# Storing the second feed-forward layer's weights unsplit, splitting left-over probabilities in two steps, and pooling one batch's values on TensorE

## The chip, the cores and the metric

The kernel runs on one core of a Trainium2 chip. The metric is the device time of one execution in microseconds (us); lower is better. TensorE (PE) multiplies matrices into PSUM, VectorE (DVE), ScalarE (ACT) and GpSimd (POOL) work on elements, and SyncE (SP) issues most DMAs from one queue, in order.

## The reference

Eight batches of 8 heads, 576 tokens and 64 dimensions each; keys and values are averaged over groups of 8 tokens before the attention. Then two feed-forward layers over all 4608 tokens.

```python
k_p = k.reshape(B, H, Sp, pool, D).mean(axis=3)
v_p = v.reshape(B, H, Sp, pool, D).mean(axis=3)
attn = softmax(scale * q @ k_p.T)
x = (attn @ v_p) reshaped to 4608 x 512
h = x @ w_in                       # 512 -> 2048
x = (s * relu(h)**2 + b) @ w_out   # 2048 -> 512
gate = sigmoid(x @ w_gate)         # 512 -> 1536
val = x @ w_val
out = (gate * val) @ w_out2        # 1536 -> 512
```

The weights arrive as 64-bit floats.

## The kernel before

Matrix products in 32-bit precision are made of three products of a rounded part and a remainder: `split(hi, lo, src, eng)` writes `hi` with an ACT copy (L55) and `lo = src - hi` with a subtraction (L56) on DVE or POOL. A product then takes three matmuls for each 128 rows (hi by lo, hi by hi, lo by hi).

**Start and attention.** Tokens go in units of 256. `scores` multiplies queries by pooled keys and leaves the difference from the maximum (L385, L386, both read PSUM on DVE); `norm` divides by the sum on POOL (L405); `left` splits the 8 left-over probabilities of each head into four slices, by two ACT copies (L412) and two DVE subtractions (L414); `turn` transposes on PE (L430, L436); `values` multiplies by the values (L448 to L451). Pooling of keys and values is a tree of POOL additions (`add`, L284; the last step of keys is L298), for batch 0 alone a sum of identity matmuls on PE (`pool_v_pe`, L326). Attention steps are spread over the first layer by a table `events`.

**First layer.** A loop over 144 steps: 9 blocks of 512 tokens by 16 slices of the hidden dimension. A step multiplies into `hps` (`emit_h`, L211 to L213) and accumulates a step two back into `acc` (`emit_x`, L242 to L244): 24 matmuls of 512 columns. In the first block the step also turns the 64-bit words of `w_in` and `w_out` into 32-bit floats: `convert` is one ACT row (L80) and three DVE rows (L81, L82, L83) for a slice, and a split on POOL follows.

**Preparation of the second layer.** From step 18 on, `prep_w2` does the same for the gate, value and output weights, one of nine parts per step, 12 slices in all. A load (`load64`, L67) takes one of three `raw` buffers; a store (L142) of a finished piece waits at the head of the SP queue until POOL has written it, and a `raw` buffer that a store reads is free for the next load only after it. Seven operand matrices (gate and value halves and four sums and differences, L187) leave for DRAM already split, as hi and lo.

**Second layer.** Two token blocks at a time, four pairs, then one block left over. `fetch_w7` loads the seven operands of a slice (L652) into one of two buffers, as soon as the matmuls on that buffer two slices back are done. `first_half` and `second_half` make seven products, 42 matmuls, with additions on DVE out of PSUM (L667), a sigmoid on ACT (L678), a multiplication (L679) and a split; `emit_o` multiplies by the output weights, 12 matmuls. PE's order is the program's order from step 16 on; the other engines' orders come from a scheduler.

Of the kernel before, what the change touches and what calls it, by code (L numbers as in the profile page):

```python
# [19 lines left out]
def pooled_attention_two_ffn(ctx, tc, q, k, v, v_left, w_in, w_out, s_in, b_in, w_gate, w_val, w_out2, out):  # L20
# [40 lines left out]
    w7d = [dram.tile([128, 2, 8 * 256], F32, name=f"w7d{m}") for m in range(M2)]  # L61
# [77 lines left out]
    def store_later():  # L139
        while later:  # L140
            dst, t = later.pop(0)
            nc.sync.dma_start(out=dst, in_=t.bitcast(F32))  # L142
# [18 lines left out]
    def store_split(dst, raw, src):  # L161
        n = src.shape[1]
        t = raw.rearrange("p (two f) -> p two f", two=2)[:, :, :n]
        split(t[:, 0].bitcast(F32R), t[:, 1].bitcast(F32R), src, nc.gpsimd)
        later.append((dst, t))

    def raw_tile():
        return rawp.tile([128, 1024], I32, tag="raw", name="raw")

    def prep_w2(m, part):  # L170
        h0, h1 = slice(0, 256), slice(256, 512)
        if part == 0:
            prep["g"] = load64(w_gate[m])
        elif part == 1:
            prep["v"] = load64(w_val[m])
        elif part == 2:
            raw = prep["g"]
            prep["gt"] = convert(raw, cv_tile())
            store_split(w7d[m][:, :, 256:768], raw, prep["gt"])
        elif part == 3:  # L180
            prep["vt"] = convert(prep["v"], cv_tile())
            store_split(w7d[m][:, :, 0:256], raw_tile(), prep["vt"][:, h0])
        elif part == 4:
            gt, vt, c = prep["gt"], prep["vt"], cv_tile().bitcast(F32)
            for o, a, b_, op in ((c[:, h1], gt[:, h0], vt[:, h0], ALU.subtract), (vt[:, h0], vt[:, h0], vt[:, h1], ALU.add),
                                 (c[:, h0], vt[:, h0], gt[:, h0], ALU.subtract), (gt[:, h1], gt[:, h1], c[:, h0], ALU.subtract)):
                nc.gpsimd.tensor_tensor(out=o, in0=a, in1=b_, op=op)  # L187
            prep["c"] = c
        elif part == 5:
            store_split(w7d[m][:, :, 768:1280], prep["v"], prep["vt"])  # L190
        elif part == 6:
            store_split(w7d[m][:, :, 1280:1792], raw_tile(), prep["c"])
        elif part == 7:
            store_split(w7d[m][:, :, 1792:2048], raw_tile(), prep["gt"][:, h1])
            prep["o"] = load64(w_out2[m])
        else:
            store_split(wo2d[m], prep["o"], convert(prep["o"], cv_tile()))
# [617 lines left out]
```

## Time and profile before

| | |
|---|---|
| median of 3 runs | 1815.9 us (1811.99 to 1817.01) |
| profiled execution, its own time | 1814.27 us |
| its span | 1812.5 us |
| mean granted TensorE clock | 0.985 |
| busy: PE, DVE, ACT, POOL | 96%, 53%, 38%, 20% |

The span runs from the first to the last instruction. A busy share is an average over stages that differ: the start and the conversion of the first layer's weights (to about 165 us), the rest of the first layer (to about 990 us), and the second layer.

### The profile page before, as it was taken

The page shows a single profiled execution, that of the slowest core. Times are in us where ns is not written, and L with a number is a line of the kernel's source. Part 1 is how long each engine was busy: PE and PEld are TensorE (multiplying, and loading weights), DVE is VectorE, ACT ScalarE, POOL GpSimd, SP SyncE. Part 2 cuts the span into 40 slices and gives each one's busy share as a digit, 9 for nine tenths or more (in the row PEclk, how much of TensorE's full clock was granted, in tenths as well). Part 3 has the DMA queues.
Part 4 walks back from the last instruction along what each step waited for, and adds up shares of the span by engine and source line. Part 5 has one row for each costly group of instructions (what it writes and reads, how often), then busy time and mean ns, then how long its engine had stood idle before and what let it go on. Part 6 is the DMA issues. An engine that isn't in the chain of part 4 may idle for free.

```text
span 1812.5 us, 21425 instructions
## 1 busy us (share of the span) xinstructions
PE 1741.0 (96%) x8032; PEld 1445.5 (80%) x8032; DVE 965.1 (53%) x1527; ACT 693.9 (38%) x1222; POOL 367.1 (20%) x395
## 2 busy tenths in 40 slices
PE   5788999999998989999999999999999999999999
PEld 4576877788887878888888888888888888888887
DVE  7997756656456665545352544455445544554111
ACT  2566544454454545445453222222222222222111
POOL 5754624406053241403000000000000000000000
PEclk7899999999999999999999999999999999999999
DMA  6676745747275553725345555855585558555764
GB/s 239 237 240 209 259 166 184 261 134 252 95 256 186 197 201 132 271 94 175 105 151 197 192 178 204 284 197 185 192 284 199 201 178 289 202 197 173 262 227 150
DMA packets 103095, 364.21 MB, mean 201 GB/s; under 512 B 10192, under 2 KB 17360, under 8 KB 102992
## 3 DMA queue, kind: packets, MB, share of 16 engines
q1 hardware_dynamic: 99792, 352.36, 56.7%
q0 software_dynamic: 3200, 10.49, 1.8%
q8 instruction: 63, 1.03, 0.2%
q14 instruction: 40, 0.33, 0.1%
HBM read 304.09 MB, written 58.72 MB: 200 GB/s over the span
## 4 chain that ended last, share of the span: by engine, by line
PE 73%; DVE 9%; DMA 8%; POOL 5%; issue 3%; ACT 2%; SPq 0%; POOLq 0%; DVEq 0%; ACTq 0%
PE acc L719 5%; PE pc L663 5%; PE pc L661 5%; PE acc L717 5%; PE pc L662 5%; PE acc L718 5%; PE hps L211 4%; PE hps L213 4%; PE hps L212 4%; PE acc L242 4%; PE pb L661 4%; PE pb L663 4%; PE pb L662 4%; PE acc L243 4%; PE acc L244 4%; DMA raw<-in 4%
## 5 line engine op out<-in xcount | busy, mean ns | idle before, releaser
L667 DVE TENSOR_TENSOR wk<-pc,wk 128x512 f32<-128x512 f32 x192 | 132.4, 690 | 240.7 <-PE pc L663 240.6
L211 PE MATMUL hps<-xl,wi 128*128 128x512 f32 (+1 forms) x584 | 236.8, 406 | 7.2 <-ACT wi L55 4.4
L242 PE MATMUL acc<-gl,woh 128*128 128x512 f32 x576 | 227.0, 394 | 11.0 <-DVE gl L56 11.0
L213 PE MATMUL hps<-xh,wi 128*128 128x512 f32 (+1 forms) x584 | 229.9, 394 | 0.0
L56 DVE TENSOR_TENSOR gl<-g,gh 128x512 fp32r<-128x512 f32 x204 | 160.2, 785 | 130.7 <-ACT gh L55 124.3
L212 PE MATMUL hps<-xh,wi 128*128 128x512 f32 (+1 forms) x584 | 229.3, 393 | 0.0
L244 PE MATMUL acc<-gh,wol 128*128 128x512 f32 x576 | 225.6, 392 | 0.0
L243 PE MATMUL acc<-gh,woh 128*128 128x512 f32 x576 | 225.5, 392 | 0.0
L55 ACT ACTIVATE gh<-g 128x512 fp32r<-128x512 f32 x204 | 128.2, 628 | 144.9 <-DVE g L679 142.1
L219 DVE TENSOR_TENSOR g<-g 128x512 f32<-128x512 f32 x128 | 101.7, 795 | 142.1 <-ACT g L215 142.0
L678 ACT ACTIVATE g<-pb 128x512 f32<-128x512 f32 x60 | 35.8, 597 | 347.7 <-PE pb L663 347.7
L661 PE MATMUL pc<-xo,w 128*128 128x512 f32 x432 | 168.0, 389 | 0.0
L662 PE MATMUL pc<-xo,w 128*128 128x512 f32 x432 | 168.0, 389 | 0.0
L663 PE MATMUL pc<-xo,w 128*128 128x512 f32 x432 | 168.0, 389 | 0.0
L568 POOL DMA_DIRECT2D cv<-x2d x36 | 19.5, 542 | 724.5 <-DMA out<-eo 338.3
L220 ACT ACTIVATE g<-g,b_sb,s_sb 128x512 f32<-128x512 f32 x144 | 117.1, 814 | 99.6 <-DVE g L219 98.4
L215 ACT ACTIVATE g<-hps 128x512 f32<-128x512 f32 x144 | 85.1, 591 | 154.5 <-PE hps L213 153.4
L242 PEld LDWEIGHTS acc<-gl,woh 128*128 128x128 f32 x576 | 108.8, 189 | 35.9 <-DVE gl L56 13.9
L211 PEld LDWEIGHTS hps<-xl,wi 128*128 128x128 f32 x584 | 112.5, 193 | 28.8 <-ACT wi L55 4.6
L213 PEld LDWEIGHTS hps<-xh,wi 128*128 128x128 f32 x584 | 111.8, 191 | 23.9
L661 PE MATMUL pb<-xo,w 128*128 128x512 f32 x336 | 130.7, 389 | 0.0
L662 PE MATMUL pb<-xo,w 128*128 128x512 f32 x336 | 130.7, 389 | 0.0
(109 smaller groups left out, 3331.0 us busy)
## 6 DMA issues: line engine op xcount, KB each, us to landing
w<-w7d SPq DMA_DIRECT2D x48, 1792.0 KB, 7.7
wi<-w1d SPq DMA_DIRECT2D x128, 512.0 KB, 3.7
wo<-wo2d SPq DMA_DIRECT2D x108, 512.0 KB, 4.4
raw<-in SPq DMA_DIRECT2D x68, 512.0 KB, 4.8
w7d<-raw SPq DMA_DIRECT2D x36, 512.0 KB, 3.6
w<-w7d SPq DMA_DIRECT2D x12, 1280.0 KB, 6.6
kv<-in SPq DMA_DIRECT2D x24, 512.0 KB, 6.0
kv<-in SPq DMA_DIRECT2D x16, 576.0 KB, 4.3
```

The costliest lines, as they stand in the source:

```text
L55: nc.scalar.activation(out=hi, in_=src, func=ACTF.Copy)
L56: eng.tensor_tensor(out=lo, in0=src, in1=hi.bitcast(F32), op=ALU.subtract)
L211: nc.tensor.matmul(out=ps[:, f], lhsT=hi[:, kk], rhs=c[:, kk, f], start=kk == 0, stop=False)
L212: nc.tensor.matmul(out=ps[:, f], lhsT=hi[:, kk], rhs=a[:, kk, f], start=False, stop=False)
L213: nc.tensor.matmul(out=ps[:, f], lhsT=lo[:, kk], rhs=a[:, kk, f], start=False, stop=kk == KD - 1)
L242: nc.tensor.matmul(out=acc[j][d], lhsT=hi[:, f], rhs=gl, start=m == 0, stop=False)
L243: nc.tensor.matmul(out=acc[j][d], lhsT=hi[:, f], rhs=gh, start=False, stop=False)
L244: nc.tensor.matmul(out=acc[j][d], lhsT=lo[:, f], rhs=gh, start=False, stop=m == M1 - 1)
L661: nc.tensor.matmul(out=ps, lhsT=w[:, 0, x, kk], rhs=r[:, 1, kk, :n], start=first and kk == 0, stop=False, skip_group_check=True)
L662: nc.tensor.matmul(out=ps, lhsT=w[:, 0, x, kk], rhs=r[:, 0, kk, :n], start=False, stop=False, skip_group_check=True)
L663: nc.tensor.matmul(out=ps, lhsT=w[:, 1, x, kk], rhs=r[:, 0, kk, :n], start=False, stop=kk == 1, skip_group_check=True)
L667: nc.vector.tensor_tensor(out=o, in0=ps, in1=b_, op=ALU.add)
```

## The change

It has three parts. The seven operands of the second layer are kept in DRAM as plain 32-bit floats: `gt` and `vt` go out straight from the converted tiles, the four sums and differences are written over the raw gate words and go out in one store, and the work is in four parts, one every second step (from step 20, the first loads at 18). `fetch_w7` now loads half the bytes and then splits what it loaded, in five pieces (two of them in the left-over block), hi on ACT and lo in place on POOL; the operands stand in another order in the buffer. `left` covers both pairs of slices with one ACT row and one DVE row of twice the elements. And the values of batch 1 are pooled on PE as those of batch 0 are.

```diff
@@ -58,7 +58,7 @@
     blocks = [(512 * i, 512) for i in range(NB)]
     NBLK = len(blocks)
     w1d = [dram.tile([128, 2, 512], F32, name=f"w1d{m}") for m in range(M1)]
-    w7d = [dram.tile([128, 2, 8 * 256], F32, name=f"w7d{m}") for m in range(M2)]
+    w7d = [dram.tile([128, 8 * 256], F32, name=f"w7d{m}") for m in range(M2)]
     wo2d = [dram.tile([128, 2, 512], F32, name=f"wo2d{m}") for m in range(M2)]
     x2d = [dram.tile([128, KD, n], F32, name=f"x2d{j}") for j, (_, n) in enumerate(blocks)]
 
@@ -139,7 +139,7 @@
     def store_later():
         while later:
             dst, t = later.pop(0)
-            nc.sync.dma_start(out=dst, in_=t.bitcast(F32))
+            nc.sync.dma_start(out=dst, in_=t if t.dtype == F32 else t.bitcast(F32))
 
     def load_wo(m):
         if m < M1:
@@ -158,43 +158,28 @@
 
     prep = {}
 
-    def store_split(dst, raw, src):
-        n = src.shape[1]
-        t = raw.rearrange("p (two f) -> p two f", two=2)[:, :, :n]
-        split(t[:, 0].bitcast(F32R), t[:, 1].bitcast(F32R), src, nc.gpsimd)
-        later.append((dst, t))
-
-    def raw_tile():
-        return rawp.tile([128, 1024], I32, tag="raw", name="raw")
-
     def prep_w2(m, part):
         h0, h1 = slice(0, 256), slice(256, 512)
         if part == 0:
             prep["g"] = load64(w_gate[m])
+            prep["v"] = load64(w_val[m])
         elif part == 1:
-            prep["v"] = load64(w_val[m])
+            prep["gt"] = convert(prep["g"], cv_tile())
+            later.append((w7d[m][:, 512:1024], prep["gt"]))
         elif part == 2:
-            raw = prep["g"]
-            prep["gt"] = convert(raw, cv_tile())
-            store_split(w7d[m][:, :, 256:768], raw, prep["gt"])
+            gt, vt, r = prep["gt"], convert(prep["v"], cv_tile()), prep["g"].bitcast(F32)
+            later.append((w7d[m][:, 0:512], vt))
+            s1, s2, s3, s4 = (r[:, 256 * x:256 * x + 256] for x in range(4))
+            for o, a, b_, op in ((s1, vt[:, h0], vt[:, h1], ALU.add), (s2, s1, gt[:, h0], ALU.subtract),
+                                 (s3, gt[:, h0], vt[:, h0], ALU.subtract), (s4, gt[:, h1], s2, ALU.subtract)):
+                nc.gpsimd.tensor_tensor(out=o, in0=a, in1=b_, op=op)
+            later.append((w7d[m][:, 1024:2048], r))
         elif part == 3:
-            prep["vt"] = convert(prep["v"], cv_tile())
-            store_split(w7d[m][:, :, 0:256], raw_tile(), prep["vt"][:, h0])
-        elif part == 4:
-            gt, vt, c = prep["gt"], prep["vt"], cv_tile().bitcast(F32)
-            for o, a, b_, op in ((c[:, h1], gt[:, h0], vt[:, h0], ALU.subtract), (vt[:, h0], vt[:, h0], vt[:, h1], ALU.add),
-                                 (c[:, h0], vt[:, h0], gt[:, h0], ALU.subtract), (gt[:, h1], gt[:, h1], c[:, h0], ALU.subtract)):
-                nc.gpsimd.tensor_tensor(out=o, in0=a, in1=b_, op=op)
-            prep["c"] = c
-        elif part == 5:
-            store_split(w7d[m][:, :, 768:1280], prep["v"], prep["vt"])
-        elif part == 6:
-            store_split(w7d[m][:, :, 1280:1792], raw_tile(), prep["c"])
-        elif part == 7:
-            store_split(w7d[m][:, :, 1792:2048], raw_tile(), prep["gt"][:, h1])
             prep["o"] = load64(w_out2[m])
         else:
-            store_split(wo2d[m], prep["o"], convert(prep["o"], cv_tile()))
+            t = prep["o"].rearrange("p (two f) -> p two f", two=2)
+            split(t[:, 0].bitcast(F32R), t[:, 1].bitcast(F32R), convert(prep["o"], cv_tile()), nc.gpsimd)
+            later.append((wo2d[m], t))
 
     g_t = {}
 
@@ -317,7 +302,7 @@
     def pool_v_pe(b, what):
 
         n = NP if what == "v" else 2
-        ps = ps_b.tile([128, n, D], F32, tag="b", name="vps")
+        ps = (ps_c if b else ps_b).tile([128, n, D], F32, tag="c" if b else "b", name="vps")
         f = ps.rearrange("p i d -> p (i d)")
         ts = [raws.pop((b, nm)) for nm in (("v0", "v1") if what == "v" else ("l",))]
         per = POOL // len(ts)
@@ -340,7 +325,7 @@
             return
         ls, vr = sums.pop((b, "l")), v3[b % 2]
         lh = at1.tile([128, 2, D], F32R, tag="lh", name="lh")
-        lm = ls if b else at1.tile([128, 2, D], F32, tag="suml", name="lm")
+        lm = ls if b > 1 else at1.tile([128, 2, D], F32, tag="suml", name="lm")
         nc.scalar.activation(out=lh, in_=ls, func=ACTF.Copy)
         nc.vector.tensor_scalar(out=lm, in0=ls, scalar1=mask[:, 1:2], scalar2=None, op0=ALU.mult)
         for g in range(4):
@@ -408,10 +393,10 @@
     def left(u, t):
         pm, pl = e_t[u, t]
         lt = at2.tile([128, H, 4, 8], F32R, tag="lt", name="lt")
-        for sl in (0, 2):
-            nc.scalar.activation(out=lt[:, :, sl], in_=pl, func=ACTF.Copy)
-        for sl in (1, 3):
-            nc.vector.tensor_tensor(out=lt[:, :, sl], in0=pl, in1=lt[:, :, sl - 1].bitcast(F32), op=ALU.subtract)
+        l4 = lt.rearrange("p h (c two) j -> p h c two j", two=2)
+        both = pl.unsqueeze(2).to_broadcast([128, H, 2, 8])
+        nc.scalar.activation(out=l4[:, :, :, 0], in_=both, func=ACTF.Copy)
+        nc.vector.tensor_tensor(out=l4[:, :, :, 1], in0=both, in1=l4[:, :, :, 0].bitcast(F32), op=ALU.subtract)
         e_t[u, t] = pm, lt
 
     def turn(u, t, part):
@@ -468,6 +453,13 @@
         at(max(p - 17, 0), pool_k, b, 0, nc.gpsimd)
         at(max(p - 15, 0), pool_k, b, 1, nc.gpsimd)
         at(max(p - 13, 0), load_kv, b, "v")
+        if b == 1:
+            at(0, load_kv, b, "l")
+            at(2, pool_v_pe, b, "v")
+            at(2, place_v, b)
+            at(3, pool_v_pe, b, "l")
+            at(3, place_left, b)
+            continue
         at(max(p - 9, 1), pool_v, b, "v", nc.gpsimd)
         at(max(p - 9, 1), load_kv, b, "l")
         at(max(p - 5, 2), pool_v, b, "l", nc.gpsimd)
@@ -615,9 +607,13 @@
                 fn(*args)
             load_wi(i + 3)
             emit_h(i)
-            x, r = divmod(i - 18, 9)
-            if i >= 18 and x < M2:
-                prep_w2(x, r)
+            x, r = divmod(i - 20, 8)
+            if i == 18:
+                prep_w2(0, 0)
+            elif i >= 20 and x < M2 and r % 2 == 0:
+                prep_w2(x, r // 2 + 1)
+                if r == 6 and x < M2 - 1:
+                    prep_w2(x + 1, 0)
             split_wi(i + 2)
             split_g(i)
             split_wo(i + 1)
@@ -647,16 +643,21 @@
         def fetch_w7(p, m):
             p, m = p + m // M2, m % M2
             if p < len(pairs):
-                a, n = (0, 5) if p == NPAIR else (1, 7)
+                a, n = (0, 4) if p == NPAIR else (1, 7)
                 w7[p, m] = w7p.tile([128, 2, 7, 2, 128], F32R, tag="w7", name="w7")[:, :, :n]
-                nc.sync.dma_start(out=w7[p, m].rearrange("p a b c d -> p a (b c d)").bitcast(F32), in_=w7d[m][:, :, 256 * a:256 * (a + n)])
+                t = w7[p, m].rearrange("p a b c d -> p a (b c d)")
+                nc.sync.dma_start(out=t[:, 1].bitcast(F32), in_=w7d[m][:, 256 * a:256 * (a + n)])
+                for f in (slice(0, 512), slice(512, 1024)) if n == 4 else (slice(256, 768), slice(1024, 1536), slice(768, 1024), slice(0, 256), slice(1536, 1792)):
+                    split(t[:, 0, f], t[:, 1, f], t[:, 1, f].bitcast(F32), nc.gpsimd)
 
         def fetch_wo(key):
             wo2[key] = wo2p.tile([128, 2, 512], F32R, tag="wo2", name="wo2")
             nc.sync.dma_start(out=wo2[key].bitcast(F32), in_=wo2d[key[2]])
 
-        def product(ps, p, m, x, first, right=None):
-            w, r, n = w7[p, m], xo[p][x if right is None else right], pairs[p][1]
+        A22, A11, A12, S1, S2, S3, S4 = range(7)
+
+        def product(ps, p, m, x, first, right):
+            w, r, n = w7[p, m], xo[p][right], pairs[p][1]
             for kk in range(2):
                 nc.tensor.matmul(out=ps, lhsT=w[:, 0, x, kk], rhs=r[:, 1, kk, :n], start=first and kk == 0, stop=False, skip_group_check=True)
                 nc.tensor.matmul(out=ps, lhsT=w[:, 0, x, kk], rhs=r[:, 0, kk, :n], start=False, stop=False, skip_group_check=True)
@@ -684,24 +685,24 @@
             n = pairs[p][1]
             b0, b1 = (ps_b.tile([128, 512], F32, tag="b", name="pb")[:, :n] for _ in range(2))
             b2, b3 = (ps_c.tile([128, 512], F32, tag="c", name="pc")[:, :n] for _ in range(2))
-            product(b0, p, m, 0, True)
+            product(b0, p, m, A11, True, 0)
             p1 = wk.tile([128, 512], F32, tag="wk", name="wk")[:, :n]
             nc.scalar.activation(out=p1, in_=b0, func=ACTF.Copy)
-            product(b1, p, m, 4, True)
...
```

POOL at the start of the first layer, before (`kv` and `s` are the raw and summed values of batch 1, the 288-wide `kv` are keys of batch 2, `wi` is a split weight slice):

```order
L405 TENSOR_TENSOR pm<-e,sm 128x512
L284 TENSOR_TENSOR kv<-kv 128x512 x3
L56 TENSOR_TENSOR wi<-cv,wi 128x512
L284 TENSOR_TENSOR kv<-kv 128x512
L284 TENSOR_TENSOR kv<-kv 128x256
L405 TENSOR_TENSOR pl<-e,sm 128x64
L405 TENSOR_TENSOR pm<-e,sm 128x512
L284 TENSOR_TENSOR kv<-kv 128x288 x2
L284 TENSOR_TENSOR s<-kv 128x256
L284 TENSOR_TENSOR s<-kv 128x128
```

POOL at the same place now:

```order
L390 TENSOR_TENSOR pm<-e,sm 128x512
L56 TENSOR_TENSOR wi<-cv,wi 128x512
L390 TENSOR_TENSOR pl<-e,sm 128x64
L390 TENSOR_TENSOR pm<-e,sm 128x512
L56 TENSOR_TENSOR wi<-cv,wi 128x512
```

The seven value additions are gone from POOL; PE has 16 more matmuls instead, and the splits follow each other closer.

The SP queue after the fifth block's end, before (`raw<-in` loads weights, `w7d` and `wo2d` are stores of prepared pieces, `wi` reloads a slice of `w_in`):

```order
L142 DMA w7d_101<-raw 256x1x512
L142 DMA w7d_101<-raw 256x1x256
L127 DMA wi<-w1d_84 128x1024
L142 DMA w7d_101<-raw 256x1x512 x2
L67 DMA raw<-in 128x1024
L127 DMA wi<-w1d_85 128x1024
L142 DMA w7d_101<-raw 256x1x256
L67 DMA raw<-in 128x1024 x2
L127 DMA wi<-w1d_86 128x1024
L142 DMA wo2d_113<-raw 128x1024
```

The SP queue at the same place now:

```order
L142 DMA w7d_102<-cv 128x512 x2
L142 DMA wo2d_113<-raw 128x1024
L67 DMA raw<-in 128x1024
L127 DMA wi<-w1d_84 128x1024
L67 DMA raw<-in 128x1024
L142 DMA w7d_102<-raw 128x1024
L127 DMA wi<-w1d_85 128x1024
L67 DMA raw<-in 128x1024
L142 DMA wo2d_114<-raw 128x1024
L142 DMA w7d_103<-cv 128x512
L127 DMA wi<-w1d_86 128x1024
L67 DMA raw<-in 128x1024
```

The first load here stood behind four stores of split pieces; now it stands behind three, of which the two from `cv` need no POOL row, and the later loads behind one or two each.

ACT where the second layer begins, before (`eo` is the last block's output of the first layer, `wk<-pb` copies the first product, `sh` is half of a split):

```order
L251 ACTIVATE eo<-acc 128x512 x2
L689 ACTIVATE wk<-pb 128x512
L678 ACT_TABLE_LOAD
L678 ACTIVATE g<-pb 128x512
L55 ACTIVATE gh<-g 128x512
L678 ACTIVATE g<-wk 128x512
L689 ACTIVATE wk<-pb 128x512
L55 ACTIVATE sh_8705<-g 128x512
L678 ACTIVATE g<-pb 128x512
```

ACT at the same place now (`w` with a number is a buffer of the seven operands):

```order
L236 ACTIVATE eo<-acc 128x512 x2
L55 ACTIVATE w_8379<-w_8379 128x512 x2
L55 ACTIVATE w_8379<-w_8379 128x256 x3
L55 ACTIVATE w_8391<-w_8391 128x512 x2
L55 ACTIVATE w_8391<-w_8391 128x256 x3
L690 ACTIVATE wk<-pb 128x512
L679 ACT_TABLE_LOAD
L679 ACTIVATE g<-pb 128x512
L55 ACTIVATE gh<-g 128x512
L679 ACTIVATE g<-wk 128x512
L690 ACTIVATE wk<-pb 128x512
L55 ACTIVATE sh_8471<-g 128x512
```

The splits of the first two slices stand between the first layer's last copies and the copy of the first product; from then on five splits stand after `sh` and before the next sigmoid.

## Rows read from the trace of the kernel before

**Rows 1.** The page's busy time of each engine, share of the span.

```profile
PE 1741.0 (96%) x8032; PEld 1445.5 (80%) x8032; DVE 965.1 (53%) x1527; ACT 693.9 (38%) x1222; POOL 367.1 (20%) x395
```

**Rows 2.** Three stages: us, busy time of each engine, granted clock, DMA.

```profile
20.00:165.00 145.00, 106.09 (x503) 85.79 (x502) 135.81 (x201) 86.66 (x168) 95.68 (x85) 0.87 0.69 232
165.00:990.00 825.00, 803.96 (x3854) 670.86 (x3853) 452.86 (x750) 404.38 (x719) 249.42 (x264) 0.99 0.54 184
990.00:1812.00 822.00, 818.57 (x3612) 677.47 (x3610) 364.07 (x546) 199.81 (x331) 17.17 (x32) 1.00 0.61 211
```

**Rows 3.** Waits from 165 to 800 us: total us, times, longest.

```profile
PE tm L430 <- DVE e L386: 11.4, 4, 4.0
...
PE sps L378 <- DVE xl L56: 4.6, 2, 3.3
...
DVE raw L81 <- DMA raw<-in: 38.7, 15, 5.0
```

**Rows 4.** Short windows around PE's longest waits, first and last of four.

```profile
220.00:240.00 20.00, 16.71 (x71) 13.64 (x70) 16.19 (x24) 10.66 (x21) 11.18 (x12) 0.91 0.67 224
...
660.00:680.00 20.00, 15.51 (x63) 12.68 (x64) 12.92 (x21) 8.39 (x16) 7.01 (x8) 0.91 0.32 119
```

**Rows 5.** Timeline of one such wait: start, length, row, idle time before.

```profile
538.15 0.34 SPq L67 DMA_DIRECT2D raw<-in  x1
...
543.64 0.43 DVE L81 TENSOR_SCALAR raw<-raw 128x512 int32<-128x512 int32 x1 [4.98 <-DMA raw<-in]
...
557.69 1.77 DVE L56 TENSOR_TENSOR gl<-g,gh 128x512 fp32r<-128x512 f32 x1
...
560.70 0.52 PE L430 MATMUL tm<-ident,pm 128*128 128x128 f32 x3 [4.02 <-DVE e L386]
```

**Rows 6.** Single lines of DVE: shortest, median and longest duration in ns.

```profile
L82 DVE SCALAR_TENSOR_TENSOR cv<-cv,raw x68: 676/688/1791, 32.7 to 840.5; 128x512 int32<-128x512 int32 x68
...
L386 DVE TENSOR_TENSOR e<-sps,mx x72: 440/448/458, 9.2 to 865.0; 128x288 f32<-128x288 f32 x72
...
L414 DVE TENSOR_TENSOR lt<-pl,lt x72: 208/610/1325, 14.7 to 869.4; 128x64 fp32r<-128x64 f32 x72
```

**Rows 7.** L82 from 20 to 165 us: busy us, mean ns.

```profile
L82 DVE SCALAR_TENSOR_TENSOR cv<-cv,raw 128x512 int32<-128x512 int32 x32 | 31.0, 975 | 1.7 <-ACT cv L80 1.2
```

**Rows 8.** POOL's value additions for batch 1, in order of time.

```profile
34.23 4.17 POOL L284 TENSOR_TENSOR kv<-kv 128x512 f32<-128x512 f32 x3
...
39.58 2.14 POOL L284 TENSOR_TENSOR kv<-kv 128x512 f32<-128x512 f32 x2
...
44.83 1.78 POOL L284 TENSOR_TENSOR s<-kv 128x256 f32<-128x256 f32 x2
```

**Rows 9.** The identity matmuls of batch 0's values: busy us, mean ns.

```profile
L326 PE MATMUL vps<-kv,ident 128*128 128x256 f32 (+1 forms) x32 | 5.9, 337 | 0.0
```

**Rows 10.** Splits of prepared pieces, both widths on POOL, the wide one on ACT.

```profile
L56 POOL TENSOR_TENSOR raw<-cv,raw 128x512 fp32r<-128x512 f32 x48 | 69.5, 1455 | 109.9 <-ACT raw L55 100.9 <-DMA raw<-in 9.0
...
L56 POOL TENSOR_TENSOR raw<-cv,raw 128x256 fp32r<-128x256 f32 x24 | 20.6, 858 | 0.4 <-ACT raw L55 0.2
...
L55 ACT ACTIVATE raw<-cv 128x512 fp32r<-128x512 f32 x48 | 30.1, 630 | 20.2 <-POOL cv L187 9.8 <-DVE cv L83 8.2 <-issue 1.7
```

**Rows 11.** The page's DMA issues: count, KB each, median us to landing.

```profile
w<-w7d SPq DMA_DIRECT2D x48, 1792.0 KB, 7.7
```

**Rows 12.** Timelines of SP and ACT over one slice of the second layer.

```profile
1023.88 0.52 SPq L652 DMA_DIRECT2D w<-w7d  x1
...
1036.12 0.52 SPq L652 DMA_DIRECT2D w<-w7d  x1
...
1033.46 0.60 ACT L678 ACTIVATE g<-pb 128x512 f32<-128x512 f32 x1 [6.73 <-PE pb L663]
```

**Rows 13.** Timelines where the second layer begins, by ACT, POOL and PE.

```profile
991.92 0.60 ACT L251 ACTIVATE eo<-acc 128x512 f32<-128x512 f32 x1 [0.76 <-PE acc L244]
...
993.59 0.54 POOL L252 DMA_DIRECT2D x2d<-eo  x1 [0.24 <-DVE eo L249]
...
992.40 0.39 PE L661 MATMUL pb<-xo,w 128*128 128x512 f32 x1
```

More of the change, by code (lines that the diff above doesn't have):

```diff
@@ L686, in first_half @@
             b2, b3 = (ps_c.tile([128, 512], F32, tag="c", name="pc")[:, :n] for _ in range(2))
-            product(b0, p, m, 0, True)
+            product(b0, p, m, A11, True, 0)
             p1 = wk.tile([128, 512], F32, tag="wk", name="wk")[:, :n]
             nc.scalar.activation(out=p1, in_=b0, func=ACTF.Copy)
-            product(b1, p, m, 4, True)
+            product(b1, p, m, S2, True, 4)
             u2 = add2(b1, p1, n)
-            product(b2, p, m, 5, True)
+            product(b2, p, m, S3, True, 5)
             u3 = add2(b2, u2, n)
-            product(b3, p, m, 2, True)
+            product(b3, p, m, S1, True, 2)
             c22 = add2(b3, u3, n)
@@ L699, in second_half @@
             n = pairs[p][1]
-            product(b0, p, m, 1, False)
-            product(b2, p, m, 3, False)
+            product(b0, p, m, A12, False, 1)
+            product(b2, p, m, A22, False, 3)
             c21 = add2(b2, u2, n)
             gated(p, m, 0, b0, c21)
-            product(b3, p, m, 6, False)
+            product(b3, p, m, S4, False, 6)
             c12 = add2(b3, u2, n)
@@ L732, in plain @@
             val = ps_c.tile([128, 512], F32, tag="c", name="pc")
-            product(gate, p, m, 1, True, 0)
-            product(gate, p, m, 2, False, 1)
+            product(gate, p, m, 2, True, 0)
+            product(gate, p, m, 3, False, 1)
             product(val, p, m, 0, True, 0)
-            product(val, p, m, 4, False, 1)
+            product(val, p, m, 1, False, 1)
             gated(p, m, 0, gate, val)
```

## The prediction

> **What bounds the kernel now.** I read the busy times first: PE is busy for 1741 of 1812.5 us [rows 1], so about 71 us are there to be won, plus what a low clock costs. The windows show where: 39 us of idle PE lie between 20 and 165 us, 21 us between 165 and 990, and 3.4 us after that [rows 2]. The second layer is therefore PE's alone: 818.57 us for 3612 matmuls is 0.227 us each, back to back. From 20 to 165 us DVE is busy for 136 of 145 us and PE for 106, with a granted clock of 0.87: DVE sets the pace there [rows 2]. In between, the table of waits says that PE waits for DVE (differences from the maximum, remainders), and that DVE itself stood 38.7 us waiting for weight loads, 15 times, up to 5.0 us [rows 3].
>
> The timeline of one case shows the order of things: a load of raw words is issued at 538.15, DVE stands 4.98 us for it until 543.64, the rows behind it come late and stretched (a remainder of `g` takes 1.77 us at 557.69), and PE then stands 4.02 us at 560.70 [rows 5]. There are four waits of 3 us or more like it, and around each the granted clock is 0.91 or 0.92 over 20 us [rows 4]; the first and the last of the four stand there. At 1.2 instead of 2.4 GHz for part of the window, that costs 0.09 x 20 = 1.8 us more each time. So from 165 to 990 us there are 21 us of idle PE and about 4 x 1.8 = 7 us of slow clock: 28 us at most.
>
> **The change, part by part.** The sum is made against the profiled execution's 1814.3 us.
>
> *Left-over probabilities.* Two DVE rows of 64 elements become one of 128. A row now takes 0.208 us at least and 0.61 in the median; the row of 288 elements takes 0.448 [rows 6]. The slope between these, 0.24 us for 224 elements, puts 128 elements at 0.28 us, and the median's surplus of 0.40 us stays once instead of twice: 0.68 us. In the stretch that DVE sets there are 16 such rows now and 8 later: 16 x 0.61 - 8 x 0.68 = 4.3 us. Bounds: 1 us if the surplus is an effect of the elements, 5.6 if the new row gets the shortest row's luck (16 x 0.61 - 8 x 0.52). The two ACT rows that become one are off the path.
>
> *Values of batch 1.* POOL loses seven additions, 8.1 us [rows 8]; PE gets 16 matmuls, for which the nearest rows, the same sum for batch 0, give 5.9 us for 32 [rows 9] (each counts twice there). They fall where PE idles anyway. What POOL's work costs DVE is seen in L82: 0.676 us at the shortest, 1.79 at the longest [rows 6], 0.975 in the mean between 20 and 165 us [rows 7], so 32 rows lose 9.6 us there while POOL is busy 95.7 us [rows 2]. L386, which reads PSUM, stays between 0.440 and 0.458 [rows 6]. A share of 8.1/95.7 of L82's 9.6 us is 0.8 us; L83, L81 and the remainders of `g` read SBUF twice or in the same manner, about three times as much together: 2.5 us in all, 0 to 4. The Trainium skill, SBUF — State Buffer, section Who interferes with whom, says that DVE and GpSimd share a pair of ports, that a DVE row with two SBUF inputs contends with a GpSimd row that reads SBUF, and that one with at most one SBUF input does not; the trace agrees, L82 with up to 1.79 us against L386's 0.458.
>
> Both parts give DVE 6.8 us back; it is busy 94% of the stretch, so I take **6 us**, bounds 1 and 9.
>
> *Preparation of the second layer.* Per slice POOL loses three wide and two narrow splits, 3 x 1.455 + 2 x 0.858 = 6.1 us [rows 10], 73 us over 12 slices; ACT loses as many copies; three raw buffers and five stores waiting on POOL become none and three, two of which wait on DVE alone. DVE's conversions are as many as before. So POOL's 249 us from 165 to 990 us [rows 2] fall to about 176, and a load is no longer queued on SP behind four stores that POOL must write. What goes is part of the 38.7 us that DVE waits for loads [rows 3] and part of the stretching; what stays is that loads still share three buffers and one queue with stores. How much PE gets no row tells. Bounds: nothing, and the 28 us from above. I take **12 us**, a little under half: the waits are few and each has slack in front of it, so shortening DVE's lateness by half removes more than half of a wait, but the pooling of keys and values (which the change leaves) is in every one of them.
>
> *Second layer, in its course.* Each load is half as large, then come five ACT copies, at most 5 x 0.63 = 3.15 us, and five POOL rows, 2 x 1.455 + 3 x 0.858 = 5.5 us [rows 10]. There are 48 such loads, and 12 with two pieces. Cover: the load of slice m+2 is issued at 1023.88 and its first product starts when the next one is issued, at 1036.12: 12.24 us [rows 12]. A load of twice the size landed after 7.7 us [rows 11]. Even with that, the first piece is ready 7.7 + 0.63 + 1.46 = 9.8 us after the issue, 2.4 us early, and the last after 7.7 + 0.63 + 5.5 = 13.8 us, for a product that is six products, 8 us, behind the first. On ACT the copies stand before the next sigmoid, which comes at 1033.46, 9.6 us after the issue [rows 12]; copies that end at 7.7 + 3.15 = 10.9 us delay it by 1.3 us, and its PSUM buffer is needed at 12.24. The cover is enough: **0 us**. DVE has nine rows there, five of which read PSUM; the other four may be stretched, into about half of the time that DVE is idle now (364 of 822 us busy [rows 2]).
>
> What speaks against this is that POOL, which now has nothing to do beside DVE there, gets 5.5 us in each slice; what that could cost is rival D below.
>
> *Second layer, its start.* Here the cover is gone. The first loads were there long before; but ACT's copies now stand behind the last `eo` copy, which ends at 992.52, and POOL's behind its last store, issued at 993.59 until 994.13, while PE would start at 992.40 [rows 13]. The first piece's lo is ready at 994.13 + 1.46 = 995.6, and the third matmul, which needs it, was due at 992.86: 2.7 us. The next piece comes 1.46 us later, just in time. ACT's copy of the first product waits for all ten copies, to 992.52 + 10 x 0.63 = 998.8 at most, some 5 us after that product's end as it is now; DVE's additions hang on it, but the buffers are written again only by the last product, 41 matmuls (9 us) after the first. **+3 us**, from 1 to 6 if the clock falls too.
>
> Sum: 1814.3 - 6 - 12 + 3 = 1799.3. The median of the runs shown is 1.6 us above the profiled execution, so **1801 us**.
>
> **The rivals.**
> *A: it is moved, not removed.* Loads still wait for stores, DVE still waits 4 to 5 us in each burst, PE's waits from 165 to 990 us stay. For it: the conversions' number and the three buffers are unchanged. Against: 73 us less POOL. Only the start and the 3 us count: 1815.9 - 6 + 3 = 1813.
> *B: all of it goes.* The waits of PE from 165 to 990 us vanish, and the slow clock with them: 1815.9 - 28 - 6 + 3 = 1785. For it: each long wait was preceded by a DVE wait of 4 to 5 us for a load. Against: smaller waits have other causes.
> *C: slower.* Loads land late in the second layer and the copies hold up the sigmoid. The point: copies and sigmoid need 3.15 + 0.6 us before 12.24, so a landing later than 8.5 us after the issue makes PE wait; 7.7 us is the median for twice the bytes [rows 11]. One microsecond beyond, 48 times, costs 48 us: 1801 + 48 = 1849.
> *D: POOL holds up DVE in the second layer.* If all nine DVE rows of a slice, 9 x 0.69 = 6.2 us by L82's median [rows 6], and POOL's 5.5 us excluded each other, a slice would need 11.7 us. That fits into 12.24 us, but not into the two slices at the head of each pair that have no `emit_o`: 42 x 0.227 = 9.5 us. Eight such slices lose 2.2 us each: 1801 + 18 = 1819. Against: five of the nine read PSUM, and the row that reads PSUM in the first layer is not stretched [rows 6]. This is the lock of the Trainium skill's SBUF page, same section, applied to every row; as that section excuses rows with one SBUF input, it speaks for a small part of D only.
>
> **How the numbers follow.** Forecast 0.56, A 0.20, B 0.12, C 0.07, D 0.05. A measurement of this kernel can tell about 0.3%, 5.4 us, from no change. Forecast and B lie below 1810.5: faster 0.68. A and D are within it: same 0.25. C: slower 0.07. The range goes from 1787 to 1814: it takes in the forecast's bounds, A, and the part of the way to B that a PE without its long waits would reach; C, D and the end of B are left out.
>
> **What would show it.** In the profile after, the first layer's weights should be converted some 6 us earlier (the last split of `w_out` on POOL), PE's waits for L386 and for `xl` should be fewer and the granted clock there above 0.91; DVE's wait for raw loads well under 38.7 us. Where the second layer starts PE should wait 2 to 4 us, once, and nowhere else behind it until the end. Loads of the operands should land in under 7.7 us. I am wrong if DVE still stands 4 to 5 us for loads in each block (A), or if PE waits at the first product of every slice (C).

## The result, and the profile after

The changed kernel takes 1794.1 us in the median of 4 runs (1790.4 to 1796.5), the kernel before 1814.7 in the same series: a ratio of 0.9885, with a 95% interval from 0.9862 to 0.9908. The forecast was 1801 us, between 1787 and 1814. The profiled execution took 1793.7 us, 20.6 less than the one of before.

Line numbers are those of each kernel: in the kernel after L415 is the transpose that was L430, L390 the product with 1/sum that was L405, L371 the difference that was L386, L237 the store of x that was L252, and L662 to L664 are the second layer's products. The page's busy times of the kernel after [rows 1]:

```profile
PE 1739.8 (97%) x8064; PEld 1446.9 (81%) x8064; DVE 937.2 (52%) x1491; ACT 774.8 (43%) x1390; POOL 550.1 (31%) x592
```

PE's work is as long as before, in a span that is 20.5 us shorter. The windows of the kernel after, with the columns and stages of [rows 2], then two of 10 us where the second layer begins:

```profile
20.00:165.00 145.00, 109.42 (x530) 89.59 (x529) 130.59 (x197) 87.03 (x164) 90.85 (x79) 0.88 0.70 237
165.00:990.00 825.00, 820.23 (x3958) 686.78 (x3957) 442.23 (x738) 384.40 (x653) 198.87 (x222) 1.00 0.49 168
990.00:1792.00 802.00, 797.80 (x3515) 659.09 (x3513) 353.24 (x531) 300.39 (x570) 255.57 (x278) 1.00 0.44 149
...
960.00:970.00 10.00, 7.82 (x33) 5.85 (x32) 2.08 (x3) 5.92 (x14) 4.17 (x6) 0.95 0.29 104
970.00:980.00 10.00, 10.00 (x40) 8.12 (x39) 3.10 (x5) 2.76 (x4) 7.14 (x9) 0.87 0.01 2
```

From 165 to 990 us 4.8 us of idle PE are left of 21, 2.2 of them at the second layer's start, which falls into this window now; the clock rounds to 1.00. PE's table of waits of the kernel after, 165 to 960 us, has one line, against the lines of PE in [rows 3]:

```profile
PE tm L415 <- POOL pm L390: 2.6, 2, 1.5
```

DVE's waits for raw loads, which I had made a cause, are nearly as long in sum, but shorter one by one (165 to 800 us, same kernel; before 38.7, 15, 5.0):

```profile
DVE raw L81 <- DMA raw<-in: 34.9, 24, 3.5
```

Where the second layer starts, its timeline [rows 13] shows the new gap: PE waits 0.53 us for ACT's copy and 1.66 us for the first lo, which POOL begins when it has issued the last store of x.

```profile
966.94 0.50 PE L662 MATMUL pb<-xo,w 128*128 128x512 f32 x1 [0.53 <-ACT w L55]
...
967.44 0.54 POOL L237 DMA_DIRECT2D x2d<-eo  x1 [0.24 <-DVE eo L234]
967.99 9.14 POOL L56 TENSOR_TENSOR w<-w 128x512 fp32r<-128x512 f32 x10
...
969.33 0.79 PE L664 MATMUL pb<-xo,w 128*128 128x512 f32 x1 [1.66 <-POOL w L56]
```

A load of the operands lands sooner (the page's DMA issues) [rows 11]:

```profile
w<-w7d SPq DMA_DIRECT2D x48, 896.0 KB, 4.4
```

To see where time is won, I take the start of ACT's first `eo` copy as the end of each block of the first layer, in this kernel and in the experiments below:

```
                      end of   gained on the kernel before, us, in block   sum of
                      block 0    1     2     3     4     5     6          1 to 8
before                 184.91
after                  186.46   5.7   6.8   0.0   7.2   7.3   0.8          27.7
e1_weights_only        185.51   5.1   6.2  -1.0   6.7   6.9   0.8          24.7
e2_small_parts_only    182.89  -0.5  -0.2   0.6   3.1   2.8   0.3           6.2
e4_pool_rows_back      185.09   0.4   3.1  -5.0   5.3   4.3  -0.9           7.2
e5_pool_memsets        185.44   5.3   7.4   0.5   7.2   7.3   0.8          28.5
e6_stores_on_pool      190.93   2.1   5.2  -1.3   0.9  -0.3  -0.2           6.3
e12_no_pool_rows       186.85   5.0   4.5   1.1   1.6   1.3   0.8          14.3
```

For the kernel after: 1.6 us lost by the end of block 0, 27.7 won in blocks 1 to 8, and 5.6 given back behind them (26.1 us ahead at the last block's end, 20.5 at the end of the span). The 27.7 us are more than PE's waits alone: each of the four long waits before had a lowered clock behind it (0.91 or 0.92 over 20 us [rows 4]), and that is gone too.

### The profile page after: what moved, and what is told of

Read it like the earlier page. It is cut to its first block, busy times and chain, and to the rows that moved or that the text cites. A ratio compares the mean times of both kernels' runs of the same rounds, so it can differ in the third digit from the quotient of the medians.

```text
span 1792.0 us, 21860 instructions
## 1 busy us (share of the span) xinstructions
PE 1739.8 (97%) x8064; PEld 1446.9 (81%) x8064; DVE 937.2 (52%) x1491; ACT 774.8 (43%) x1390; POOL 550.1 (31%) x592
## 4 chain that ended last, share of the span: by engine, by line
PE 72%; issue 4%; DMA 1%; POOL 1%; DVE 0%; ACT 0%; POOLq 0%; DVEq 0%
PE pc L664 5%; PE pc L663 5%; PE pc L662 5%; PE acc L718 5%; PE acc L720 5%; PE acc L719 5%; PE pb L664 4%; PE pb L663 4%; PE pb L662 4%; PE hps L196 4%; PE hps L198 4%; PE hps L197 4%; PE acc L227 4%; PE acc L229 4%; PE acc L228 4%
## 5 line engine op out<-in xcount | busy, mean ns | idle before, releaser
L56 POOL TENSOR_TENSOR w<-w 128x512 fp32r<-128x512 f32 x264 | 254.4, 996 | 505.2 <-ACT w L55 481.7
L198 PE MATMUL hps<-xh,wi 128*128 128x512 f32 (+1 forms) x584 | 227.4, 389 | 0.0
L197 PE MATMUL hps<-xh,wi 128*128 128x512 f32 (+1 forms) x584 | 227.1, 389 | 0.0
L204 DVE TENSOR_TENSOR g<-g 128x512 f32<-128x512 f32 x128 | 97.9, 765 | 150.3 <-ACT g L200 150.3
L662 PE MATMUL pc<-xo,w 128*128 128x512 f32 x432 | 168.1, 389 | 0.0
L664 PE MATMUL pc<-xo,w 128*128 128x512 f32 x432 | 168.1, 389 | 0.0
L55 ACT ACTIVATE w<-w 128x512 fp32r<-128x512 f32 x264 | 113.3, 503 | 100.4 <-DMA w<-w7d 100.4
L664 PE MATMUL pb<-xo,w 128*128 128x512 f32 x336 | 131.6, 392 | 1.7 <-POOL w L56 1.7
L662 PE MATMUL pb<-xo,w 128*128 128x512 f32 x336 | 131.3, 391 | 0.5 <-ACT w L55 0.5
L663 PE MATMUL pb<-xo,w 128*128 128x512 f32 x336 | 131.2, 390 | 0.0
```

Source lines behind the costliest of these rows:

```text
L55: nc.scalar.activation(out=hi, in_=src, func=ACTF.Copy)
L56: eng.tensor_tensor(out=lo, in0=src, in1=hi.bitcast(F32), op=ALU.subtract)
L197: nc.tensor.matmul(out=ps[:, f], lhsT=hi[:, kk], rhs=a[:, kk, f], start=False, stop=False)
L198: nc.tensor.matmul(out=ps[:, f], lhsT=lo[:, kk], rhs=a[:, kk, f], start=False, stop=kk == KD - 1)
L662: nc.tensor.matmul(out=ps, lhsT=w[:, 0, x, kk], rhs=r[:, 1, kk, :n], start=first and kk == 0, stop=False, skip_group_check=True)
L663: nc.tensor.matmul(out=ps, lhsT=w[:, 0, x, kk], rhs=r[:, 0, kk, :n], start=False, stop=False, skip_group_check=True)
```

## The experiments

Theory: the preparation is what gains, because POOL's rows that read SBUF stretched DVE's rows. Rivals: it gains because loads no longer stand behind stores; because POOL's other rows come sooner; or the two small parts have a good part in it.

**Which part gains.** e1 is the change without the small parts, e2 the small parts alone on the kernel before, e3 the change with the old `left`, e11 the change with batch 1's values on POOL.

```diff
-        both = pl.unsqueeze(2).to_broadcast([128, H, 2, 8])
-        nc.scalar.activation(out=l4[:, :, :, 0], in_=both, func=ACTF.Copy)
-        nc.vector.tensor_tensor(out=l4[:, :, :, 1], in0=both, in1=l4[:, :, :, 0].bitcast(F32), op=ALU.subtract)
+        for sl in (0, 2):
+            nc.scalar.activation(out=lt[:, :, sl], in_=pl, func=ACTF.Copy)
+        for sl in (1, 3):
+            nc.vector.tensor_tensor(out=lt[:, :, sl], in0=pl, in1=lt[:, :, sl - 1].bitcast(F32), op=ALU.subtract)
...
-        if b == 1:
-            at(0, load_kv, b, "l")
-            at(2, pool_v_pe, b, "v")
...
```

(e3 has the first half, e11 the second, e1 both, e2 the reverse of both on the kernel before.)

> The change with its two small parts undone: left-over probabilities split in four rows and batch 1's values pooled on POOL, as before; only the weights' preparation and their split per load remain. Theory (the preparation is what gains between 165 and 990 us, the small parts gave nothing by the end of the first block): 1792 to 1797 us, against 1794 for the whole change. Rival (the small parts' relief of DVE, one row of about 0.6 us less for each of 36 pieces of 128 tokens, is a good part of the gain between 165 and 990): 1800 to 1806 us.

> The kernel before with the two small parts alone: left-over probabilities split in two rows and batch 1's values pooled on PE; the second layer's weights are prepared, stored and loaded as before. Theory (only the preparation gains): 1812 to 1816 us, within 0.3% of the kernel before. Rival (the small parts relieve DVE along the whole first layer): 1803 to 1808 us. By the term on record (6 us won before 165 us) it would be 1809.

> The change with the left-over probabilities in four rows again, the rest as it is. Theory (the rows are hidden): 1792 to 1797 us. By the term on record the 4.3 us come back: about 1798. Rival (DVE rows of the left-over probabilities stretch every burst): 1800 or more.

> The change with batch 1's values pooled by POOL again, the rest as it is (left-over probabilities in two rows). By the term on record the 2.5 us come back: about 1797 us. Theory (the early stretch does not turn DVE's relief into time): 1793 to 1796 us. With the runs before, this completes the four combinations of the two small parts under the new preparation.

Measured, medians in us, with the ratio to the kernel before and its interval:

```
preparation  left in two rows  values on PE
new          yes               yes    after  1794.07  0.9885 [0.9862, 0.9908]
new          no                no     e1     1795.05  0.9896 [0.9877, 0.9914]
new          no                yes    e3     1797.94  0.9906 [0.9888, 0.9925]
new          yes               no     e11    1791.53  0.9867 [0.9853, 0.9882]
old          yes               yes    e2     1808.49  0.9972 [0.9954, 0.9989]
```

The preparation alone gives the whole gain. Alone on the kernel before the small parts are worth 5.7 us (the profile shows 6.0 won in blocks 4 and 5); beside the new preparation, about 1. What the first theory said of e2 (no change) is wrong; the two gains overlap. The 1809 us that the term on record gave for e2 is met by luck: 2.0 us are won by the end of block 0 and 6.0 in blocks 4 and 5. e3 stands at the 1798 us of the term on record, just above the theory's 1792 to 1797; e11 came out below both of its forecasts. In both pairs the merged rows read as a gain (1795.05 to 1791.53, 1797.94 to 1794.07) and the values on PE as a loss (1791.53 to 1794.07, 1795.05 to 1797.94) of 2.5 to 3.9 us, but the intervals overlap: a hint, not a finding.

**What in the preparation gains.** e4 puts POOL rows back that nothing waits for; e5 keeps POOL as busy with rows that read nothing.

```diff
+            if i >= 20 and x < M2 and r % 2:
+                if r == 1:
+                    prep["d"] = cv_tile().bitcast(F32)
+                s = wo[0][0].bitcast(F32)
+                for n in {1: (512,), 3: (256, 256), 5: (512,), 7: (512,)}[r]:
+                    nc.gpsimd.tensor_tensor(out=prep["d"][:, :n], in0=s[:, :n], in1=s[:, :n], op=ALU.subtract)
...
# e5 has in place of the last three lines
+                for _ in range(3):
+                    nc.gpsimd.memset(prep["d"], 0.0)
```

> The change with as many POOL rows put back into the preparation as it removed: per slice three subtractions of 512 and two of 256 elements a partition, from a resident weight tile into a scratch tile, on which no store and no load waits. Their results are not used. Theory POOL (the removed work stretched DVE's rows, and POOL's other rows came late): most of the preparation's gain is lost, 1808 to 1816 us. Theory stores (the gain is that loads no longer stand behind stores that wait for POOL): still 1794 to 1798 us. In between, 1800 to 1806, both have a share.

> The change with POOL kept as busy as by the rows put back in the run before, but by rows that read nothing: 12 memsets of 128x512 a slice into the same scratch tile (0.47 us each, back to back, at the kernel's start; 12 x 12 x 0.47 = 68 us, against 67.4 us of rows put back). Theory ports (what costs is that POOL's reads stretch DVE's rows with two SBUF inputs): 1794 to 1799 us. Theory queue (what costs is that POOL's other rows, the pooling of keys and the products with 1/sum, come later behind the added ones): 1805 to 1813 us.

Measured: e4 1810.9 us, 0.9981 [0.9969, 0.9992], as theory POOL has it; e5 1791.85 us, 0.9878 [0.9863, 0.9893], a little under the range of theory ports. The window from 165 to 990 us of e4:

```profile
165.00:990.00 825.00, 806.37 (x3874) 673.22 (x3873) 465.35 (x721) 378.20 (x640) 256.12 (x270) 0.99 0.49 167
```

DVE's two conversion rows in e4 (shortest, median, longest ns, 190 to 960 us):

```profile
L82 DVE SCALAR_TENSOR_TENSOR cv<-cv,raw x36: 677/972/1566, 191.0 to 809.4; 128x512 int32<-128x512 int32 x36
...
L83 DVE SCALAR_TENSOR_TENSOR cv<-raw,cv x36: 677/1098/1776, 195.3 to 810.4; 128x512 int32<-128x512 int32 x36
```

The same window of e5:

```profile
165.00:990.00 825.00, 821.57 (x3966) 687.35 (x3965) 449.29 (x740) 387.11 (x656) 268.96 (x366) 1.00 0.50 169
```

The same two rows in e5:

```profile
L82 DVE SCALAR_TENSOR_TENSOR cv<-cv,raw x36: 677/682/1608, 191.4 to 788.5; 128x512 int32<-128x512 int32 x36
...
L83 DVE SCALAR_TENSOR_TENSOR cv<-raw,cv x36: 675/684/1115, 194.9 to 789.5; 128x512 int32<-128x512 int32 x36
```

The reader should set the fifth busy time, POOL's, against the third, DVE's. POOL is busier in e5 (269 us) than in e4 (256), its rows stand in the same steps, and yet the medians of L82 and L83 stay at 0.68 us and nothing is lost. With reads the medians go to 0.97 and 1.10 us, DVE is busy 16 us longer than in e5, and 17 of the 20 us are gone. So POOL's occupation costs nothing here; its reads do. The Trainium skill, SBUF — State Buffer, section Who interferes with whom, exempts GpSimd rows that don't read SBUF from the lock on the shared ports: e5 agrees. The rows put back stand in other steps than those removed, so the 17 us are not the removed rows' price. In the kernel before, the same two rows are as short as in e5 (same window):

```profile
L82 DVE SCALAR_TENSOR_TENSOR cv<-cv,raw x36: 678/688/1681, 191.4 to 840.5; 128x512 int32<-128x512 int32 x36
...
L83 DVE SCALAR_TENSOR_TENSOR cv<-raw,cv x36: 672/684/1666, 194.0 to 841.2; 128x512 int32<-128x512 int32 x36
```

So the rows taken away mostly did not stand beside these two, as those of e4 do. What they stretched is told by the next runs.

**From the other side, on the kernel before.** e6 takes the stores of finished weight pieces off SP; e12 takes the POOL rows away, and its stores then wait for ACT instead of POOL. Its remainders are not computed.

```diff
# e6
-            nc.sync.dma_start(out=dst, in_=t.bitcast(F32))
+            nc.gpsimd.dma_start(out=dst, in_=t.bitcast(F32))
# e12, in store_split
-        split(t[:, 0].bitcast(F32R), t[:, 1].bitcast(F32R), src, nc.gpsimd)
+        for x in range(2):
+            nc.scalar.activation(out=t[:, x].bitcast(F32R), in_=src, func=ACTF.Copy)
```

> The kernel before with the stores of all finished pieces of weights issued from POOL's queue, behind the rows that write them, so that no load stands behind a store on SP; three raw buffers as before, and some 76 issues of about 0.54 us (the issue of a load on POOL) more on POOL, 41 us. Theory stores (loads stood behind stores): 1800 to 1807 us. Theory POOL (its load is what costs): 1813 to 1822 us, since its load grows.

> The kernel before with the five POOL splits a slice in the second layer's preparation replaced by a second ACT copy each (the remainders that leave for DRAM are not computed; their place holds a copy of the operand). Five stores a slice, three raw buffers, split loads in the second layer and the two small parts are as before, so nothing of the change is in it but POOL's relief, 36 rows of 512 and 24 of 256. Theory POOL rows (all of the preparation's gain): the blocks end 24 to 28 us earlier by the last one, and as the second layer's loads are split already no time is given back at its start: 1786 to 1791 us. Theory both (with POOL's rows put back 19 of 26 us were lost, and the other 7 are due to fewer stores and whole loads): 1793 to 1798 us. Theory stores alone: 1810 to 1816.

Measured: e6 1813.93 us, 1.001 [0.9999, 1.0021]; e12 1801.48 us, 0.992 [0.9902, 0.9938]. e6 is no clean test of the loads' queue: the stores of `w_in`'s pieces moved too, and block 0 ends 6 us later, which blocks 1 and 2 win back. e12 met none of its three forecasts: half of the gain (14.3 of 27.7 us in blocks 1 to 8). PE's waits in e12, 550 and 656 us:

```profile
550.68 1.08 PE L431 MATMUL tm<-ident,pm 128*128 128x128 f32 x4 [4.05 <-DVE e L387]
...
655.92 1.09 PE L431 MATMUL tm<-ident,pm 128*128 128x128 f32 x4 [4.23 <-DVE e L387]
```

Blocks 1 and 2 are won by taking POOL's rows away (9.5 of 12.5 us, and e4 loses 8.9 of them again). Blocks 4 and 5 are not (2.9 of 14.5 us, and e4 keeps 9.6): the wait of [rows 5] and its like one block on are still there. They are gone in e4, with the rows back (where another, of 4.84 us, costs block 3 its 5.0), and shorter in e2 (2.2 and 2.8 us). Such a wait may be made of several delays at once; the parts do not add up, in any case.

The stretching alone does not set the gain. The windows from the end of block 0 to that of block 8, in which PE does the same work, of the kernel before, e1, e12, the kernel after and e4:

```profile
184.91:990.56 805.65, 784.61 (x3761) 654.57 (x3760) 444.28 (x734) 392.22 (x699) 241.91 (x256) 0.99 0.54 184
...
185.51:966.50 780.99, 776.09 (x3759) 649.64 (x3758) 428.00 (x733) 364.48 (x640) 176.19 (x196) 1.00 0.50 171
...
186.85:978.22 791.37, 779.46 (x3761) 652.61 (x3760) 410.99 (x734) 420.51 (x772) 147.81 (x184) 1.00 0.55 188
...
186.46:964.41 777.95, 775.36 (x3760) 650.10 (x3759) 422.49 (x705) 361.52 (x612) 177.07 (x196) 1.00 0.50 172
...
185.09:983.50 798.41, 781.96 (x3761) 653.39 (x3760) 456.43 (x705) 363.57 (x612) 245.00 (x256) 0.99 0.49 167
```

With as many rows (733 or 734), DVE is busy 33 us less in e12 and 16 us less in e1, so the removed rows did stretch DVE's; but e12, with twice the relief, wins 14.3 us and e1 24.7. And e4's rows cost DVE 34 us against the kernel after, twice what their removal had given in e1. DVE's waits for raw loads differ too (165 to 800 us, e12; 38.7, 15, 5.0 before [rows 3] and 34.9, 24, 3.5 after):

```profile
DVE raw L81 <- DMA raw<-in: 43.9, 21, 4.4
```

What ended the two waits of blocks 4 and 5 in the change (three stores for five, loads in another step, or a slice every 8 steps instead of 9, which moves the conversions against the scores) no run separates, and e12 does not tell POOL's reads from its holding up of the stores. It stays open.

**The second layer's start.** e7 issues the last stores of x on SP; e8 also cuts the first slice finer and puts its first remainders on DVE; e9 is e8 with the stores on POOL.

```diff
# e7, e8
-                (nc.gpsimd if j == NBLK - 1 else nc.sync).dma_start(out=x2d[j][:, d, :], in_=eo)
+                nc.sync.dma_start(out=x2d[j][:, d, :], in_=eo)
# e8, e9, in fetch_w7
+                if (p, m) == (0, 0):
+                    cut = (slice(256, 512), slice(1024, 1280), slice(1280, 1536), slice(768, 1024), slice(512, 768), slice(0, 256), slice(1536, 1792))
...
+                    split(t[:, 0, f], t[:, 1, f], t[:, 1, f].bitcast(F32), nc.vector if (p, m) == (0, 0) and x < 3 else nc.gpsimd)
```

> The change with the last block's four stores of x issued from SP instead of POOL. Theory (the second layer's first lo waits behind those issues on POOL): PE's wait of 1.66 us for the POOL split falls below 1 us, 1791 to 1793 us. Rival (the split takes its 0.9 us behind the copies anyway, and SP's loads of weights now stand behind the stores): 1794 to 1796 us.

> The run before, and the second layer's first slice cut finer: its first operand alone in the first piece, the next two pieces of one operand each, and the remainders of these three on DVE instead of POOL. Theory (the 4.4 us at the start are the first slice's splits and the clock that falls behind the gap): PE's gap at the first product under 1 us, the clock there 1.00, 1789 to 1792 us. Rival (ACT's copies set the start, or DVE's additions come late behind the three rows): 1793 to 1796 us.

> The change with only the second layer's first slice cut finer (its first operand alone, then two pieces of one operand, the remainders of these three on DVE); the last block's stores of x stay on POOL. Theory (with the loads early again, the 1.66 us wait for the POOL split goes, and with it the slow clock behind it): 1789 to 1792 us. Rival (the gap in front of the first product, for ACT's copy, and the course of the layer behind it keep the time): 1793 to 1796 us.

None met a forecast; all three come out 4 to 6 us above the change: 1799.79 us, 0.9918 [0.9904, 0.9931]; 1798.14 us, 0.9911 [0.9897, 0.9925]; 1798.63 us, 0.9903 [0.9886, 0.9921]. The intervals still touch the change's, but the traces show the loss: from block 8's end to the first `eo` copy of the second layer the change loses 4.3 us on the kernel before, e7, e8 and e9 lose 9.2, 8.9 and 7.9. In e7 the first loads of the layer now stand behind the stores in SP's queue. The timeline of the kernel after by SP, then of e7 by SP, ACT and PE:

```profile
942.33 0.90 SPq L649 DMA_DIRECT2D w<-w7d  x2
...
965.62 0.46 SPq L649 DMA_DIRECT2D w<-w7d  x1
...
971.58 2.07 ACT L55 ACTIVATE w<-w 128x512 fp32r<-128x512 f32 x5 [5.76 <-DMA w<-w7d]
...
972.26 0.79 PE L662 MATMUL pb<-xo,w 128*128 128x512 f32 x1 [6.40 <-ACT w L55]
```

The loads are issued 23 us later, and PE waits 6.40 us instead of 0.53. With POOL's queue the stores were out of the loads' way, which I had read only as a delay of POOL. In e9 the cure meets what e4 and e5 showed (DVE's rows on the tile `w`: shortest, median and longest ns):

```profile
L56 DVE TENSOR_TENSOR w<-w x3: 414/418/7846, 968.5 to 969.2; 128x256 fp32r<-128x256 f32 x3
```

The timelines of e9 by POOL and by PE, right behind:

```profile
969.45 7.29 POOL L56 TENSOR_TENSOR w<-w 128x256 fp32r<-128x256 f32 x9
...
977.09 0.80 PE L667 MATMUL pc<-xo,w 128*128 128x512 f32 x1 [5.09 <-DVE w L56]
```

Two of DVE's three rows take 0.41 us. The third, begun at 969.2, ends 0.3 us behind POOL's train of nine rows (969.45 + 7.29 = 976.74), and PE stands 5.09 us for it.

**Where the early gain went.** In the kernel after a transpose at 91.05 us waits 4.56 us for a DVE row (L371), which I read as the row that frees its PSUM buffer; before, no wait stands there. e10 puts batch 1's sums into the other PSUM pool.

```diff
-        ps = (ps_c if b else ps_b).tile([128, n, D], F32, tag="c" if b else "b", name="vps")
+        ps = ps_b.tile([128, n, D], F32, tag="b", name="vps")
```

> The change with batch 1's value sums in the PSUM pool that batch 0's sums and the hidden blocks use (ps_b), instead of the pool of the scores, transposes and attention outputs (ps_c). Theory (the sums' place in ps_c makes the transposes at 91 us wait 4.6 us for their PSUM buffer, which eats the time that DVE got back): the end of the first block at 181 to 183 us instead of 183 to 186, the whole 1790 to 1792. Rival (the early stretch is held by the ring of load, conversion and buffer, whatever the PSUM buffer): 1793 to 1796 us.

Measured: 1790.45 us, 0.9863 [0.9847, 0.988], the fastest of all; the intervals of it and of the change overlap, so that it is faster than the change is not shown. The wait is gone (at 86.07 us it is 1.21 us), and block 0 ends at 183.32 us, a little later than the theory's 181 to 183. The seven kernels that have the change's code in block 0 unaltered (after, e2, e4, e5, e7, e8, e9) end it anywhere from 182.89 to 187.14 us, so one profile each cannot settle 3 us there.

## Why the prediction came out as it did

*Early stretch, -6 us: wrong.* The lower bound was 1 us won; block 0 ended 1.6 us later, in the seven kernels from 2.0 us earlier to 2.2 later. Three steps failed. "Values of batch 1": the stretch of L82 and L83 did not fall with POOL's 8.1 us (31.0 and 30.0 us before, 30.2 and 31.3 after), so the share of 8.1/95.7 was no measure; which rows of POOL stand beside DVE's may count for more. Whether the new rows of PE "fall where PE idles anyway" no run shows (PE is busy 3.3 us longer in the stretch [rows 2]); their sums' PSUM buffer probably made the 4.56 us wait, which is gone in e10. "Left-over probabilities": from 20 to 165 us 14 rows of 9.3 us became 7 of 6.9, about 0.99 us each and not 0.68, so 2.4 us instead of 4.3. And "DVE sets the pace" was too simple: it is busy 5.2 us less and PE did not go faster; in this profile of the kernel after DVE waits 7.1 us for raw loads from 20 to 187 us, before 1.8. The last split of `wol` on POOL ends at 163.1 instead of 166.8 us, 3.7 and not 6 us sooner.

*Preparation, -12 us: right in direction, off in size.* 27.7 us were won, the bound of 28 and the amount of rival B. The step that failed is "a little under half", with its reason that the pooling of keys and values would remain in every wait. What remains are two waits for POOL's products with 1/sum (`pm`), 2.6 us. Of the two causes that I named, DVE's waits for loads hardly fell in sum (38.7 to 34.9 us), though the longest did; the stretching fell by 16 us (e1), but is not what sets the gain (e12). Blocks 1 and 2 go mostly with POOL's rows, blocks 4 and 5 mostly with the rest of the preparation; by which path stays open.

*Second layer's start, +3 us: right in place, somewhat small.* The gap is 2.2 us (2.7 worked out). Behind it the clock was 0.95 and 0.87 in two windows of 10 us, 10 x (0.05 + 0.13) = 1.8 us, so 4.0 together, inside the stated 1 to 6. The part for the clock is luck: in five other runs the same gap left the clock at 1.00.

*Second layer's course, 0: nearly right.* About 1 to 1.6 us go there. No wait stands at the first product of a slice, and the one wait of PE above 0.25 us is 0.26 us, at 1668 us, for output weights; loads land after 4.4 us, and the copies fit. C is refuted in this profile. D too: POOL is busy 256 us behind 990 us, DVE 353, and PE stays at 797.80 of 802 us.

So 1.6 - 27.7 + 4.0 + 1.6 = -20.5 us stands against -6 - 12 + 3 = -15: 7.6 us of the early gain are missing, the preparation gives 15.7 more, and 2.6 more are given back behind it. That the sum came within 7 us of the measured time is partly luck: two misses of 10.2 us together stand against one of 15.7 the other way.

## What to carry to other kernels

Count POOL's rows that read SBUF beside DVE's rows with two SBUF inputs, not POOL's busy share: the same occupation by memsets cost nothing here, by reads 17 us. But do not take DVE's relief for time won: twice the relief won little more than half as much here. A long stall may go whole when only a part of what delays it goes, or stay, so bound such a gain by the whole stall and do not add up the parts. Work that is moved onto an idle engine brings its buffers and its queue along: stores issued ahead of a load cost 5 us at the second layer's start (e7), and a sum in the PSUM pool of the transposes probably a wait.

## What was unexpected of the hardware

A DVE subtraction of 256 elements took 7.85 us instead of 0.41 beside nine POOL rows that came without a pause (e9). The Trainium skill's SBUF page, same section, says, of DVE's 2-port modes, that whoever issues first gets the shared pair for the whole instruction and the other is blocked. Here DVE's row has two SBUF inputs; by the profile it began 0.27 us ahead of the train and was held until the train's end all the same, so it got no turn between the nine rows either.

The same gap at the second layer's start, 0.53 us and then 1.65 or 1.66 us for POOL, left the clock at 1.00 in e3, e4, e5, e10 and e11; in the kernel after and in e1 it fell (0.95 and 0.87 in two windows of 10 us; 0.83 in one). The layer's first block loses 4.3 us in these two and 2.8 in the five: what a short gap costs in clock differs from one profiled execution to the next.
